# A fused attention, max-out and PReLU kernel: another order of the gate units in the three planned batches

## The chip, the cores and the metric

The kernel runs on one core of a Trainium2 chip. The metric is the device time of one execution in microseconds. It was measured in three runs of the kernel before: 749.68, 751.30 and 750.57 us, median 750.57 us. The trace shown here is of one further execution of the same kernel.

Five engines work side by side, each through its own list of instructions in the order in which they were issued: TensorE (PE in the rows; its weight loads are PEld), VectorE (DVE), ScalarE (ACT), GpSimd (POOL) and SyncE (SP), which here only starts transfers. They wait for each other by semaphores.

## What is computed

```python
def _attn_ref(q, k, v):                      # 4 batches, 8 heads, 576 tokens, 64 wide
    scores = np.matmul(q, k.transpose(0, 1, 3, 2)) / np.sqrt(D)
    rel = pos[:, None] - pos[None, :]
    mask_local = (rel >= 0) & (rel < 32)                                  # heads 0 to 3
    mask_strided = (rel >= 0) & (pos[None, :] % 32 == pos[:, None] % 32)  # heads 4 to 7
    ...
    return softmax(np.where(masks, scores, -1e9)) @ v
def _moe_ref(x, w1, w2, w3, w_out):          # 2304 tokens, 512 -> 768 -> 512
    h = np.maximum(np.maximum(x @ w1, x @ w2), x @ w3)
    return h @ w_out
def _moe2_ref(x, w_in, w_out, alpha):        # 512 -> 2048 -> 512
    h = x @ w_in
    return (np.maximum(h, 0) + alpha * np.minimum(h, 0)) @ w_out
```

The three run one after the other; the output of the attention, seen as 2304 tokens of 512 features, is the input of the second.

## The kernel before

The program has three stretches. In the first (0 to some 316 us of the trace) the attention of all four batches, the max-out net of batches 0, 1 and 2, and the preparation of all weights are woven together. In the second (`last_net`) the max-out net of batch 3 runs. In the third the PReLU net runs over all tokens. Only the first has its order changed.

**Units of the max-out net.** A batch has 576 tokens in two halves of 288 (`hf` 0 and 1). A *gate unit* `(hf, f, g)` multiplies the 288 tokens of a half with one block of 128 columns (`f`, six of them) of one of the three gate weights (`g`): 12 matmuls at line 580, of 128x128 by 288 columns. After the unit g = 0, ACT copies the result to a tile `t` (L667); after g = 1 and g = 2, DVE takes the greater of result and `t` (L670). Then ACT casts `t` into a tile `h` (L676) and DVE makes its low part (L259). A *mix unit* multiplies all six `h` of a half with 128 columns of the output weights: 18 matmuls at line 602; a half has four. Its result `xo` is copied by ACT (L650) and stored by SP (L613). So a batch has 36 gate units (432 matmuls) and 8 mix units (144).

**Attention.** A batch's attention comes in eight steps. Each has scores (L317 on PE), a mask and a maximum (L325, DVE), exponentials (L332, ACT), a reciprocal (L343, L344, DVE), a scaling (L354 on ACT or L356 on DVE), transposes (L367, PE), a copy (L256, ACT or DVE), values (L392, PE) and a split into `x` (L256 and L259). The attention of batch b + 1 runs between the gate and mix units of batch b.

**Weights.** Each block of weights comes in as double precision (`raw`, L437 on SP), is made into single precision words (L451 on ACT; L455 and L457 on DVE) and split into a high and a low part (L256 on ACT, L259 on DVE). In batch 0 the 18 gate weights are made just ahead of their use. Later ones are sums of blocks (L524, L553, L563) and are written back by SP (L489) through three buffers.

**What sets the order.** Each piece of work is a task with engines, estimated costs, a position, needs and the rings of buffers that it takes from: 8 PSUM banks, 4 tiles `t`, 12 tiles `h`, 11 tiles `x`, 3 store buffers and so on. `Weave.plan` goes through a made-up time with these costs and, at each step, takes the task with the lowest position among those that could start soon; a change of kind of work on PE counts 100 ns in it. So the built order of all engines follows from the positions. `net_tasks` gives the gate and mix units of batch b the positions `b * NUNITS + n`, with n counted through a list: `GATES_FIRST` for batch 0, `GATES` for batch 1, `GATES_THEN` for batch 2. An entry `(hf, f)` stands for its three gate units, a `None` for the four mix units of the next half.

**After the planned part.** `last_net` begins with sums on DVE (L704, L710) into tiles that take over the memory of the store buffers, then the gate units of four blocks `f` (144 matmuls at L580, their maxima at L591), with `make(0)` to `make(7)` between them (L214: eight operands, named T1 to T4). Then come products of six matmuls (L753) on these operands; the fifth one takes T4.

Of the kernel before, what the change touches and what calls it, by code (L numbers as in the profile page):

```python
# [163 lines left out]
def attention_maxout_prelu_kernel(  # L164
# [442 lines left out]
    def store_x2(b, hf, dc, xo):  # L607
        first = b * S + hf * HALF
        done = 0
        while done < HALF:  # L610
# [4 lines left out]

    GATES_FIRST = [(0, 0), (0, 1), (1, 0), (0, 2), (1, 1), (0, 3), (1, 2), (0, 4), (1, 3), (0, 5),
                   (1, 4), None, (1, 5), None]
    GATES = [(0, 0), (0, 1), (0, 2), (1, 0), (0, 3), (0, 4), (1, 1), (0, 5), (1, 2),  # L620
             None, (1, 3), (1, 4), (1, 5), None]
    GATES_THEN = [what for what in GATES if what] + [None, None]
    GATES_LAST = [(hf, f) for f in range(2 * NP // 3) for hf in range(2)]

    def units(gates):
# [281 lines left out]
    for b in range(B - 1):  # L907
        net_tasks(b, (GATES_FIRST, GATES, GATES_THEN)[b])
    weave.run()
# [436 lines left out]
```

## Time and profile before

| | |
|---|---|
| runs | 749.68, 750.57, 751.30 us; median 750.57 us |
| the profiled execution | 749.45 us in all; its span, first to last instruction, 747.7 us |
| PE busy | 732.9 us (98% of the span), 5560 matmuls |
| DVE busy | 640.3 us (86%) |
| ACT busy | 464.5 us (62%) |
| granted TensorE clock | 1.000, mean over the span |

The profiled execution is 1.12 us below the median of the runs. Busy time is the time in which an engine had an instruction in work; matmuls overlap, so a full PE is not one at its peak, and the distance from one matmul's start to the next one's says more than the length of one.

### The profile page before, as it was taken

The numbers are of one execution on the slowest core, as the hardware profiler recorded it, in microseconds if no ns is written. First come the engines' busy times: TensorE is split into PE (matmuls) and PEld (weight loads), VectorE is DVE, ScalarE is ACT, GpSimd is POOL, SyncE is SP. The second block draws the span as 40 slices with busy tenths as digits, with TensorE's granted clock in tenths as the row PEclk, the third lists the DMA queues.
The fourth block names the chain that finished last, engine by engine and source line by source line (L and its number), as shares of the span: only waits on it lengthen the run. The fifth ranks groups of instructions, "written<-read, shape, count | busy, mean of one in ns | idle before, by whom it ended". The sixth has DMA issues, their size and how long they took to land.

```text
span 747.7 us, 16003 instructions
## 1 busy us (share of the span) xinstructions
PE 732.9 (98%) x5560; PEld 710.3 (95%) x5560; DVE 640.3 (86%) x1711; ACT 464.5 (62%) x1254; POOL 28.7 (4%) x42
## 2 busy tenths in 40 slices
PE   5899999999999999999999999999999999999998
PEld 4699999999999999999999999999999999999997
DVE  4899999899898999478868898888989888988896
ACT  5987889568684788423345666634666654556571
POOL 1000000000000000023500000000000000000000
PEclk9999999999999999999999999999999999999999
DMA  7477769996999765779899789999789999867362
GB/s 248 155 244 227 234 206 337 342 342 244 323 318 340 252 219 208 253 267 332 306 319 400 266 293 332 383 401 372 265 286 316 364 401 369 289 236 254 118 201 77
DMA packets 88929, 211.96 MB, mean 283 GB/s; under 512 B 11024, under 2 KB 41232, under 8 KB 88848
## 3 DMA queue, kind: packets, MB, share of 16 engines
q1 hardware_dynamic: 88848, 210.94, 80.4%
q8 instruction: 44, 0.72, 0.4%
q14 instruction: 37, 0.30, 0.1%
HBM read 154.80 MB, written 56.10 MB: 282 GB/s over the span
## 4 chain that ended last, share of the span: by engine, by line
PE 94%; ACT 2%; DMA 2%; DVE 1%; issue 0%; SPq 0%; ACTq 0%; DVEq 0%
PE bank L580 24%; PE ph L1185 23%; PE po L986 15%; PE bank L602 10%; PE bank L753 4%; PE po L992 4%; PE ph L986 3%; PE bank L317 3%; PE bank L392 2%; PE bank L367 2%; PE po L996 2%; ACT e L332 1%; DMA wh<-w 1%; DMA k<-in_kTs 0%; PE po L1185 0%; DMA wo<-w 0%
## 5 line engine op out<-in xcount | busy, mean ns | idle before, releaser
L1185 PE MATMUL ph<-x,w 128*128 128x384 f32 x990 | 200.1, 337 | 0.0
L580 PE MATMUL bank<-x,w 128*128 128x288 f32 x1440 | 197.5, 296 | 0.0
L580 PEld LDWEIGHTS bank<-x,w 128*128 128x128 f32 x1440 | 191.8, 188 | 2.1
L1185 PEld LDWEIGHTS ph<-x,w 128*128 128x128 f32 x990 | 166.3, 188 | 1.0
L986 PE MATMUL po<-w,g 128*128 128x256 f32 x936 | 135.6, 281 | 0.0
L986 PEld LDWEIGHTS po<-w,g 128*128 128x128 f32 x936 | 130.1, 189 | 0.4
L1191 DVE TENSOR_TENSOR c<-ph,c 128x384 f32<-128x384 f32 x165 | 89.5, 555 | 30.5 <-PE ph L1185 27.4
L979 ACT CAST g<-c 128x384 fp32r<-128x384 f32 x93 | 47.0, 505 | 91.1 <-DVE c L1169 51.7
L602 PE MATMUL bank<-h,w 128*128 128x288 f32 x576 | 79.4, 297 | 0.0
L602 PEld LDWEIGHTS bank<-h,w 128*128 128x128 f32 x576 | 76.9, 188 | 0.9
L256 ACT CAST w<-word 128x512 fp32r<-128x512 f32 x100 | 58.0, 590 | 24.8 <-DMA wh<-w 7.9
L332 ACT ACTIVATE e<-e,nm 96x128 f32<-96x128 f32 (+2 forms) x176 | 68.1, 396 | 6.1 <-DVE nm L325 5.9
L259 DVE TENSOR_TENSOR w<-word,w 128x512 fp32r<-128x512 f32 x100 | 63.4, 642 | 9.2 <-ACT w L256 8.9
L1129 ACT ACTIVATE c<-c 128x384 f32<-128x384 f32 x96 | 50.5, 526 | 32.9 <-DVE c L1191 31.8
L1130 ACT ACTIVATE c<-c,nalpha 128x384 f32<-128x384 f32 x96 | 59.2, 617 | 3.1
L1134 DVE SCALAR_TENSOR_TENSOR c<-c 128x384 f32<-128x384 f32 x96 | 53.1, 553 | 6.1 <-ACT c L1130 6.1
L980 DVE TENSOR_TENSOR g<-c,g 128x384 fp32r<-128x384 f32 x96 | 53.0, 552 | 0.9 <-ACT g L979 0.5
L451 ACT ACTIVATE word<-raw 128x512 f32<-128x512 f32 x56 | 37.6, 682 | 14.6 <-DMA raw<-in_w 10.8
L980 DVE TENSOR_TENSOR g<-k,g 128x384 fp32r<-128x384 f32 x72 | 37.2, 558 | 7.5 <-ACT g L979 7.5
L992 PE MATMUL po<-w,g 128*128 128x512 f32 x120 | 43.0, 397 | 0.0
L457 DVE SCALAR_TENSOR_TENSOR word<-raw,word 128x512 uint32<-128x512 uint32 x56 | 38.8, 692 | 1.9
L1169 DVE TENSOR_TENSOR k<-c 128x384 f32<-128x384 f32 x72 | 37.9, 551 | 0.0
(107 smaller groups left out, 939.1 us busy)
## 6 DMA issues: line engine op xcount, KB each, us to landing
w<-wh SPq DMA_DIRECT2D x72, 512.0 KB, 5.3
raw<-in_w SPq DMA_DIRECT2D x50, 512.0 KB, 5.1
w<-wo SPq DMA_DIRECT2D x48, 512.0 KB, 5.8
w<-wp SPq DMA_DIRECT2D x36, 512.0 KB, 6.4
wh<-w SPq DMA_DIRECT2D x24, 512.0 KB, 5.0
xd<-xst SPq DMA_DIRECT2D x28, 384.0 KB, 3.2
x<-xd SPq DMA_DIRECT2D x28, 384.0 KB, 8.2
ws<-w SPq DMA_DIRECT2D x12, 512.0 KB, 5.4
```

What stands on the lines that cost most here:

```text
L256: (nc.scalar.copy if e == "ACT" else nc.vector.tensor_copy)(out_, in_)
L259: nc.vector.tensor_tensor(out=out_, in0=x, in1=y, op=ALU.subtract)
L332: nc.scalar.activation(tl[ek][:nq, j, i, :nk], tl[ek][:nq, j, i, :nk], AF.Exp, bias=tl["nm", u][:nq, j, i:i + 1], scale=-1.0, accum_out=tl ...
L580: nc.tensor.matmul(acc, words["gate", f, g][:, wi, cc * P:(cc + 1) * P], xt[b, cc, hf][:, xi, :], start=n == 0, stop=n == 3 * NCC - 1)
L602: nc.tensor.matmul(acc, words["mix", f][:, wi, dc * P:(dc + 1) * P], st["h", hf, f][:, xi, :], start=n == 0, stop=n == 3 * NF1 - 1)
L980: return g, lambda: nc.vector.tensor_tensor(out=g[:, 1], in0=x, in1=g[:, 0].bitcast(F32), op=ALU.subtract)
L986: nc.tensor.matmul(bank[:, NH * half:NH * (half + 1)], g[:, gi, t * P:(t + 1) * P], w[:, wi, off:off + NH], start=first and i == 0, stop=l ...
L992: nc.tensor.matmul(bank.rearrange("p (s n) -> p s n", n=NH), g[:, 0, t * P:(t + 1) * P], w[:, :, off:off + NH], start=first, stop=last)
L1130: nc.scalar.activation(a, a, AF.Copy, scale=nalpha[:, f:f + 1])
L1134: nc.vector.scalar_tensor_tensor(out=a, in0=h, scalar=0.0, in1=a, op0=ALU.max, op1=ALU.add)
L1185: nc.tensor.matmul(bank, words["h", n, i][:, wi, off + c * P:off + (c + 1) * P], x2h[blk, k, c][:, xi, :], start=m == 0, stop=m == 5)
L1191: nc.vector.tensor_tensor(out=out_, in0=bank, in1=other, op=ALU.add)
```

## The change

The three lists of the planned batches are written in another order. In `GATES_FIRST` and `GATES` a `None` stood between gates of the second half; now both `None` stand last. `GATES_THEN` had both last already, and has another order of the gates alone.

```diff
-    GATES = [(0, 0), (0, 1), (0, 2), (1, 0), (0, 3), (0, 4), (1, 1), (0, 5), (1, 2),
-             None, (1, 3), (1, 4), (1, 5), None]
+    GATES = [(0, 0), (1, 0), (0, 1), (0, 2), (1, 1), (0, 3), (1, 2), (1, 3), (0, 4), (0, 5), (1, 4),
+             (1, 5), None, None]
```

The number of matmuls on PE (5210 as issued), and the set of transfers on SP (555), are the same in both programs. From the last mix unit on, PE's list is the same in both. Line numbers after the lists are greater by one in the changed kernel.

PE's list where batch 1 begins, which is the end of batch 0's mix and the first gates of batch 1. Before:

```order
L602 MATMUL bank<-h,w 128x288 x72
L580 MATMUL bank<-x,w 128x288 x96
L367 MATMUL bank<-ident,e 108x108 x6
L580 MATMUL bank<-x,w 128x288 x48
L367 MATMUL bank<-ident,e 126x126 x4
L392 MATMUL bank<-pt,v 64x108 x6
L580 MATMUL bank<-x,w 128x288 x48
L392 MATMUL bank<-pt,v 64x126 x4
L367 MATMUL bank<-ident,e 108x108 x6
L317 MATMUL bank<-k,q 126x126 x4
L580 MATMUL bank<-x,w 128x288 x48
```

And now:

```order
L602 MATMUL bank<-h,w 128x288 x72
L580 MATMUL bank<-x,w 128x288 x60
L317 MATMUL bank<-k,q 108x108 x6
L580 MATMUL bank<-x,w 128x288 x36
L317 MATMUL bank<-k,q 126x126 x4
L580 MATMUL bank<-x,w 128x288 x12
L367 MATMUL bank<-ident,e 108x108 x6
L580 MATMUL bank<-x,w 128x288 x36
L367 MATMUL bank<-ident,e 126x126 x4
L392 MATMUL bank<-pt,v 64x108 x6
L317 MATMUL bank<-k,q 108x108 x6
L580 MATMUL bank<-x,w 128x288 x48
```

The first scores of the next batch stood within the mix of batch 0 before; now they stand by themselves between gates.

DVE's list in batch 0 between the fifth weight block (w_885) and the sixth (w_928 before, w_926 now). Before:

```order
L259 TENSOR_TENSOR w_885<-word_852,w_885 128x512
L259 TENSOR_TENSOR h_906<-t_760,h_906 128x288
L455 TENSOR_SCALAR word_908<-word_908 128x512
L457 SCALAR_TENSOR_TENSOR word_908<-raw_850,word_908 128x512
L670 TENSOR_TENSOR t_789<-bank_910,t_789 128x288
L259 TENSOR_TENSOR w_928<-word_879,w_928 128x512
```

And now:

```order
L259 TENSOR_TENSOR w_885<-word_852,w_885 128x512
L671 TENSOR_TENSOR t_789<-bank_887,t_789 128x288
L259 TENSOR_TENSOR h_905<-t_760,h_905 128x288
L259 TENSOR_TENSOR w_926<-word_879,w_926 128x512
L259 TENSOR_TENSOR h_930<-t_789,h_930 128x288
```

The two steps that make the words of the seventh block stood ahead of the sixth block's low part, and stand behind it now.

SP's list at the end of the planned part: the stores of the last weight sums (wo7, wp) and of the mix results of batch 2 (x2). Before, xo_4917 is the fifth of the batch's eight results and xo_4971 the seventh:

```order
L489 DMA wo7_0_120<-w_4938 128x1024
L489 DMA wo7_1_121<-w_4942 256x1x256
L489 DMA wp2_3_173<-w_4942 256x1x256
L489 DMA wo7_1_121<-w_4966 256x1x256
L489 DMA wp0_3_165<-w_4966 256x1x256
L613 DMA x2_3_71<-xo_4917 128x96
L613 DMA x2_4_72<-xo_4917 128x192
L613 DMA x2_3_71<-xo_4944 128x96
L613 DMA x2_4_72<-xo_4944 128x192
L613 DMA x2_3_71<-xo_4971 128x96
L613 DMA x2_4_72<-xo_4971 128x192
L489 DMA wp1_3_169<-w_4995 256x1x256
```

And now, where xo_4930 is the sixth result and xo_4989 the last:

```order
L613 DMA x2_3_71<-xo_4930 128x96
L613 DMA x2_4_72<-xo_4930 128x192
L489 DMA wo7_0_120<-w_4960 128x1024
L489 DMA wo7_1_121<-w_4987 256x1x256
L489 DMA wp2_3_173<-w_4987 256x1x256
L489 DMA wo7_1_121<-w_5009 256x1x256
L489 DMA wp0_3_165<-w_5009 256x1x256
L613 DMA x2_3_71<-xo_4962 128x96
L613 DMA x2_4_72<-xo_4962 128x192
L613 DMA x2_3_71<-xo_4989 128x96
L613 DMA x2_4_72<-xo_4989 128x192
L489 DMA wp1_3_169<-w_5019 256x1x256
```

The five stores from wo7_0 on stood ahead of the fifth result, and stand behind the sixth now.

## Rows read from the trace of the kernel before

**Rows 1.** The page: the span, busy time by engine, the chain that ended last.

```profile
span 747.7 us, 16003 instructions
...
PE 732.9 (98%) x5560; PEld 710.3 (95%) x5560; DVE 640.3 (86%) x1711; ACT 464.5 (62%) x1254; POOL 28.7 (4%) x42
...
PE 94%; ACT 2%; DMA 2%; DVE 1%; issue 0%; SPq 0%; ACTq 0%; DVEq 0%
```

**Rows 2.** Windows: stretch, its length, busy us (instructions) by engine, clock, DMA share, GB/s.

```profile
25.00:50.00 25.00, 22.69 (x206) 19.89 (x207) 23.78 (x104) 25.00 (x102) 0.00 (x0) 1.00 0.67 218
...
125.00:150.00 25.00, 25.00 (x193) 25.00 (x192) 20.33 (x46) 15.73 (x43) 0.00 (x0) 1.00 0.94 333
```

**Rows 3.** PE's waits, whole span: us in total, times, longest us.

```profile
PE bank L317 <- DMA k<-in_kTs: 5.9, 2, 4.5
...
PE bank L367 <- DVE e L356: 1.9, 3, 0.7
...
PE bank L317 <- ACT pt L256: 0.3, 1, 0.3
```

**Rows 4.** PE's timeline, 38 to 310 us: start, length, merged instructions.

```profile
103.71 1.55 PE L317 MATMUL bank<-k,q 64*96 64x128 f32 x24
105.19 5.06 PE L602 MATMUL bank<-h,w 128*128 128x288 f32 x36
...
131.47 12.86 PE L580 MATMUL bank<-x,w 128*128 128x288 f32 x96
144.17 0.72 PE L367 MATMUL bank<-ident,e 108*108 108x108 f32 x6
144.66 6.62 PE L580 MATMUL bank<-x,w 128*128 128x288 f32 x48
151.12 0.59 PE L367 MATMUL bank<-ident,e 126*126 126x126 f32 x4
...
160.81 6.62 PE L580 MATMUL bank<-x,w 128*128 128x288 f32 x48
167.36 0.90 PE L317 MATMUL bank<-k,q 64*96 64x128 f32 x12
168.19 1.88 PE L580 MATMUL bank<-x,w 128*128 128x288 f32 x12
```

**Rows 5.** PE's timeline where it waits within batch 1.

```profile
212.81 0.71 PE L317 MATMUL bank<-k,q 64*126 64x126 f32 x8 [0.26 <-ACT pt L256]
```

**Rows 6.** PE's timeline, the first 240 matmuls of gates.

```profile
38.45 32.11 PE L580 MATMUL bank<-x,w 128*128 128x288 f32 x240
```

**Rows 7.** DVE's timeline in batch 0: the low parts of blocks five and six.

```profile
48.58 0.69 DVE L259 TENSOR_TENSOR w<-word,w 128x512 fp32r<-128x512 f32 x1
49.18 0.45 DVE L259 TENSOR_TENSOR h<-t,h 128x288 fp32r<-128x288 f32 x1
...
51.10 0.68 DVE L259 TENSOR_TENSOR w<-word,w 128x512 fp32r<-128x512 f32 x1
```

**Rows 8.** DVE's timeline where the last net begins, up to its last operands.

```profile
312.42 0.43 DVE L259 TENSOR_TENSOR w<-word,w 128x256 fp32r<-128x256 f32 x1 [1.48 <-ACT w L256]
319.17 1.56 DVE L704 TENSOR_TENSOR xs<-x 128x288 f32<-128x288 f32 x4 [6.33 <-DMA wp<-w]
...
336.90 0.82 DVE L214 TENSOR_TENSOR x<-t,x 128x288 fp32r<-128x288 f32 x2
```

**Rows 9.** PE's timeline there: the last net's gates and its first products.

```profile
316.24 19.20 PE L580 MATMUL bank<-x,w 128*128 128x288 f32 x144
335.28 10.00 PE L753 MATMUL bank<-x,w 128*128 128x288 f32 x74
```

**Rows 10.** SP's timeline there: the issue of the last weight store.

```profile
316.61 0.52 SPq L489 DMA_DIRECT2D wp<-w  x1
```

**Rows 11.** DMA issues, whole span: count, KB each, median us to landing.

```profile
w<-wp SPq DMA_DIRECT2D x36, 512.0 KB, 6.4
...
wp<-w SPq DMA_DIRECT2D x24, 256.0 KB, 3.2
```

More of the change, by code (lines that the diff above doesn't have):

```diff
@@ L614, in store_x2 @@
             done += nn
-    GATES_FIRST = [(0, 0), (0, 1), (1, 0), (0, 2), (1, 1), (0, 3), (1, 2), (0, 4), (1, 3), (0, 5),
-                   (1, 4), None, (1, 5), None]
-    GATES = [(0, 0), (0, 1), (0, 2), (1, 0), (0, 3), (0, 4), (1, 1), (0, 5), (1, 2),
-             None, (1, 3), (1, 4), (1, 5), None]
-    GATES_THEN = [what for what in GATES if what] + [None, None]
+    GATES_FIRST = [(0, 0), (1, 0), (0, 1), (1, 1), (0, 2), (0, 3), (1, 2), (1, 3), (0, 4), (1, 4), (0, 5),
+                   (1, 5), None, None]
+    GATES = [(0, 0), (1, 0), (0, 1), (0, 2), (1, 1), (0, 3), (1, 2), (1, 3), (0, 4), (0, 5), (1, 4),
+             (1, 5), None, None]
+    GATES_THEN = [(0, 0), (0, 1), (0, 2), (1, 0), (1, 1), (0, 3), (1, 2), (0, 4), (1, 3), (1, 4), (0, 5),
+                  (1, 5), None, None]
     GATES_LAST = [(hf, f) for f in range(2 * NP // 3) for hf in range(2)]
```

## The prediction

> **What bounds the kernel now.** I read the page first: PE is busy for 732.9 of 747.7 us, and 94% of the chain that ended last is PE [rows 1]. The windows say where it is not: in 25 to 50 us it lacks 2.3 us, and from 50 us on the windows are full, as the one at 125 to 150 us, at a granted clock of 1.00, the upper of the two levels (2.4 GHz) [rows 2]. DVE has 20 to 24 of 25 us there, so it is close to being a second bound, but it is not the one that is waited for. The list of PE's waits confirms this: its largest entry is 5.9 us for the first keys, and the only wait after the first gate at 38.45 us [rows 6] is one of 0.26 us for the copy `pt` [rows 3, 5]. The change leaves everything ahead of that gate as it is. So in the planned part, 38 to 316 us, PE has 0.26 us to win from better timing, and what the change does to the time must come from three things: how much time PE's own work takes in the new order, new waits inside the batches, and new waits at the seam to the last net. Behind the seam every engine has its old list.
>
> **PE's own work in the new order.** The matmuls are the same, but PE changes between gates or mix (288 columns, 128 rows) and attention (64 to 128 columns) at other places. The timeline prices this from one start to the next. 96 gates behind a mix and ahead of transposes take 144.17 − 131.47 = 12.70 us, 132.3 ns each [rows 4]. 48 gates with scores on both sides take 167.36 − 160.81 = 6.55 us where 48 x 132.3 ns is 6.35: two edges with scores or values cost 0.20 us, 0.10 each. 48 gates between transposes take 151.12 − 144.66 = 6.46, half of that. One step of scores alone takes 168.19 − 167.36 = 0.83 us, two in one piece 105.19 − 103.71 = 1.48: a piece that is cut in two costs 0.18 more. Now the count, from the two lists of PE between the first gate and the last net: 32 visits to attention before, 37 now. Edges with scores or values go from 43 to 53, edges with transposes stay 21. Pieces of scores go from 19 to 20, pieces of values from 19 to 20, those of transposes stay 20. So 10 x 0.10 + 2 x 0.18 = **1.36 us more** (for a cut of values I take the price of one of scores). The excerpt of PE's list at batch 1's start shows where: scores that shared a visit within the mix now stand alone between gates. Nothing covers this, since PE has no idle time there.
>
> The Trainium skill ("TensorE: Matmul & The Clock Gate", Single matmul latency) gives a single warm matmul (398 + N)/2.4 ns, that is, 166 ns beside its columns. Were each of the ten edges to empty the array once, the first part would be 1.66 us in place of 1.0 by that page, and the sum 0.66 us higher; the row of 48 gates has 0.10 per edge, and I go by the row.
>
> **The wait that goes.** The 0.26 us stand where scores follow two steps of transposes and need a bank back [rows 5]. In the new list these scores stand elsewhere, between gates, so **−0.26 us**.
>
> **Weights in batch 0.** Gates take 12 x 132.3 ns = 1.59 us per unit from 38.45 us on [rows 6]. In PE's lists the blocks are first used by units 0, 2, 4, 5, 7, 9, 10, 11, 13, 15, 16, 17, 21 ... before, and 0, 2, 4, 6, 7, 8, 12, 13, 14, 15, 16, 17, 24 ... now. Only the sixth is wanted earlier: at unit 8, 51.2 us, not unit 9, 52.8. Its low part ended at 51.10 + 0.68 = 51.78 [rows 7], which would be 0.6 us late. But DVE's list has changed as well: behind the fifth block's end at 48.58 + 0.69 = 49.27 stand a maximum, an `h` (0.45 each) and then the sixth block (0.68), so it ends at 50.85, 0.4 us before it is wanted. Bounds 0 and 0.6; I take **0**. The others are wanted at the same unit or later, and what is queued behind (blocks ten to twelve, at the same units as before) keeps its pace, since DVE has lost no work and gained none.
>
> **The seam to the last net.** Here a wait is ready in the trace. DVE's first sum of the last net starts at 319.17 us, after 6.33 us without work, when a weight store has landed [rows 8], issued by SP at 316.61 [rows 10], so 2.5 us before. From there to the last operand T4, at 336.90 + 0.82 = 337.72, DVE goes through a fixed list. PE wants T4 in its fifth product: 335.28 + 4 x 6 x 0.1323 = 338.46 us [rows 9]. So the margin is 0.74 us; beyond it, PE waits as long as the store is late. In the new program SP's five stores from wo7_0 on stand behind the sixth mix result, not the fourth, and DVE's first sum waits for the last two of these five (its semaphores; the very last store now holds back a load instead). The mix ends at 316.24 and a unit takes 18 x 0.1323 = 2.38 us, so the sixth result is there at 311.5; with ACT's copy (0.4 us, an estimate from the like-sized 0.45 of DVE) and two stores ahead at 0.52 each [rows 10], the five start at 312.9 and the fifth is issued at 312.9 + 4 x 0.52 = 315.0, complete at 315.5. It lands 2.5 us later if it flies like the last one before (318.0: no later than now, nothing lost), 3.2 us later by the median of such stores (318.7), and up to 6.4 later by the slower of the two groups shown, loads of twice the size (321.9: 2.7 late, of which PE feels 2.0) [rows 11]. Behind the store DVE holds the maxima of the last net's gates, and these hold banks; but T4's margin is the first to go. I take 1.0 late, between the median and the far end because five stores follow each other closely, so **+0.3 us**, bounds 0 and 2.0.
>
> **Other waits in the batches.** Each of the 24 attention steps has its chain DVE, ACT, DVE, PE at another place among the gates. Lower bound 0 (−0.26 is counted). Upper bound: the longest wait of this kind anywhere, in the start-up where little covers it, is 0.7 us [rows 3]; one for each batch makes 2.1. In 24 steps the trace has one wait, of 0.26, so I take **0**.
>
> **Sum.** 1.36 − 0.26 + 0.3 = +1.4 us on the profiled execution's 749.45 us (span 747.7 and 1.75 around it), 750.85. The median of the runs stands 1.12 us above this execution, so **752.0 us**, 0.19% more than 750.57. 0.2%, 1.5 us, is about what a measurement of this kernel can tell from no change, so this is just within.
>
> **Rivals.**
> - *The seam decides* (chance 0.25). The stores land over 1.1 us late, so that PE waits over 0.4 us: from there on the kernel is slower by over 0.2%. At the far bound, 750.57 + 1.1 + 2.0 = 753.7. For it: the margin of 0.74 is small. Against it: DVE's sums no longer wait for the very last store.
> - *One wait in each batch* (0.15): 0.26 to 0.7 three times, 752.5 to 753.8. For it: DVE is nearly full, so that a chain that stands badly has nothing to catch up with. Against it: one such wait in three batches so far.
> - *Edges empty the array* (0.05): the dearer price of the rule above, 752.6. Against it stands the row of 48 gates.
> - *Visits cost nothing* (0.05): PE's price per edge is made up elsewhere, and only the 0.26 go: 750.3. Against it: from 50 us on PE has no idle time in which to hide anything.
> - *Faster* (0.05): consecutive units now share weights more often. If PE then skipped loads, it would gain; but it has one load for each of its 5560 matmuls [rows 1], and the program still issues each. Apart from that 0.26 us is all there is to win, and only scatter would make it more.
>
> **How the numbers follow.** My forecast as summed has 0.45; its own range is 751.3 to 752.1, +0.7 to +1.5. With the case of visits that cost nothing, 0.50 within 0.2%; with the seam, the waits and the dear edges, 0.45 slower; 0.05 faster. The range that leaves out 0.2 goes down to 750.7, into the case of free visits, and up to 753.7, the far end of the seam.
>
> **What would show it.** In the changed kernel's timeline, 48 gates between scores should again take 6.55 us, and the last net's first gate should start 1.1 us later, at 317.3. DVE's sixth low part should end before PE's ninth unit begins, with no gap in the run of 240 gates. PE should have a gap of some tenths of a us four products behind the last net's gates, and DVE's first sum should start 3 to 4 us behind PE's last-net gates (2.9 now). The prediction is wrong if PE's waits between 38 and 316 us exceed 0.5 us, if that gap exceeds 0.7, or if the gates start the last net no later than now: the last would say that edges are not what the rows make of them.

## The result, and the profile after

Six runs of the changed kernel took 755.91 to 758.78 us, median 757.18; six of the kernel before, on the same chip, 749.49 to 751.30, median 750.48. The ratio is 1.0092, interval 1.0076 to 1.0109: 6.7 us slower, where 752.0 us, within 0.2% of before, had been forecast. The profiled execution took 758.47 us, its span 756.7 us, 9.0 us more than that of [rows 1]. It stands 1.3 us above the median of its kernel and the profiled one before 1.0 below that of its own, so the profiles show some 2 us more loss than the medians.

The page of the changed kernel: span, busy time, the chain that ended last.

```profile
span 756.7 us, 16006 instructions
...
PE 737.5 (97%) x5560; PEld 713.2 (94%) x5560; DVE 639.5 (85%) x1711; ACT 464.5 (61%) x1252; POOL 28.5 (4%) x42
...
PE 85%; DMA 6%; ACT 4%; POOL 1%; DVE 1%; issue 1%; SPq 0%; ACTq 0%; DVEq 0%; POOLq 0%
```

PE was 94% of the chain and is 85%; DMA went from 2 to 6% and ACT from 2 to 4%. So somewhere the end now runs through a transfer and through ACT. PE is also *busy* 4.6 us longer with the same 5560 matmuls, so some matmuls got slower. The list of PE's waits says where the first of the two is (us in total, times, longest):

```profile
PE bank L317 <- DMA k<-in_kTs: 5.7, 2, 4.7
PE ph L1186 <- ACT xo L810: 4.1, 1, 4.1
...
PE bank L317 <- DMA k<-in_kTl: 0.4, 1, 0.4
PE bank L602 <- DVE h L741: 0.2, 1, 0.2
```

The first row answers to the first of [rows 3] and is nearly the same (5.9 there). The second is new: one wait of 4.1 us, at line 1186, for an `xo` copy of ACT. Line 1186 is the first product of the third stretch, the PReLU net; it is nowhere in the prediction. A product here is six matmuls into one PSUM bank, a part of the memory that TensorE writes its results to; the row of 12 matmuls at 394.57 holds the first two products. PE's timeline from the planned part on:

```profile
169.82 6.62 PE L580 MATMUL bank<-x,w 128*128 128x288 f32 x48
176.37 0.90 PE L317 MATMUL bank<-k,q 64*96 64x128 f32 x12
...
318.02 19.20 PE L580 MATMUL bank<-x,w 128*128 128x288 f32 x144
337.06 33.80 PE L754 MATMUL bank<-x,w 128*128 128x288 f32 x252
370.69 2.32 PE L602 MATMUL bank<-h,w 128*128 128x288 f32 x16
373.25 17.20 PE L602 MATMUL bank<-h,w 128*128 128x288 f32 x128 [0.24 <-DVE h L741]
394.57 4.21 PE L1186 MATMUL ph<-x,w 128*128 128x384 f32 x12 [4.12 <-ACT xo L810]
398.57 2.91 PE L1186 MATMUL po<-x,w 128*128 128x384 f32 x12
401.33 2.25 PE L1186 MATMUL ph<-x,w 128*128 128x384 f32 x12
```

The same place in the kernel before, which [rows 1 to 11] don't reach:

```profile
368.88 19.24 PE L602 MATMUL bank<-h,w 128*128 128x288 f32 x144
387.96 2.24 PE L1185 MATMUL ph<-x,w 128*128 128x384 f32 x12
390.04 2.24 PE L1185 MATMUL po<-x,w 128*128 128x384 f32 x12
392.12 2.24 PE L1185 MATMUL ph<-x,w 128*128 128x384 f32 x12
```

Read from start to start, these rows add up the loss. The first gate starts 0.07 us later (38.52), the last net's gates 1.78 us later than in [rows 9] (318.02), its products again 1.78 later, its mix 1.81 later. The mix takes some 0.5 us longer, with a wait of 0.24 us in it, and ends at 390.45, where a next matmul could start about 0.16 us earlier, as it does in the kernel before. Then come 4.3 us in which PE waits. And the first 24 matmuls take 401.33 − 394.57 = 6.76 us where they took 392.12 − 387.96 = 4.16: another 2.6 us. Together that is 9.2 us; the spans differ by 9.0. Windows of 2 us at this place (length, busy us and instructions of PE, PEld, DVE, ACT and POOL, granted clock, DMA share, GB/s) show what the 2.6 us are:

```profile
390.00:392.00 2.00, 0.44 (x4) 0.21 (x2) 2.00 (x6) 2.00 (x6) 0.00 (x0) 1.00 0.93 293
392.00:394.00 2.00, 0.00 (x0) 0.00 (x0) 0.53 (x2) 0.47 (x2) 0.00 (x0) 0.78 0.96 256
394.00:396.00 2.00, 1.43 (x4) 1.43 (x5) 0.00 (x0) 0.40 (x1) 0.00 (x0) 0.50 1.03 320
...
398.00:400.00 2.00, 2.00 (x8) 2.00 (x7) 0.56 (x1) 0.00 (x0) 0.00 (x0) 0.51 1.03 409
400.00:402.00 2.00, 2.00 (x13) 2.00 (x12) 1.03 (x2) 0.91 (x2) 0.00 (x0) 1.00 1.02 388
```

PE does nothing from 390.45 to 394.57, and within that idle time the granted clock falls from 1.00 to 0.50, the lower of the two levels (1.2 GHz). It stays there up to 400 us: 8 matmuls in 2 us, not 13.

Why does the *first* product wait, whose operands are ready? ACT's timeline of the changed kernel:

```profile
379.57 0.51 ACT L211 CAST x<-xs 128x384 fp32r<-128x384 f32 x1 [4.38 <-DMA xs<-x]
...
391.38 1.13 ACT L810 COPY xo<-bank 128x288 f32<-128x288 f32 x3
394.12 0.40 ACT L810 COPY xo<-bank 128x288 f32<-128x288 f32 x1 [1.61 <-DMA x<-xo]
```

And of the kernel before:

```profile
388.34 0.40 ACT L809 COPY xo<-bank 128x288 f32<-128x288 f32 x1 [0.31 <-DMA x<-xo]
390.05 0.40 ACT L809 COPY xo<-bank 128x288 f32<-128x288 f32 x1 [1.31 <-DMA x<-xo]
```

There too ACT's last copies come late: the last ends at 390.45, 2.3 us behind the mix's end at 388.12. Yet PE's first product did not wait for it. The difference is in the PSUM banks. The third stretch opens two pools of banks in place of the one that the mix used:

```python
ps_o = ctx.enter_context(tc.tile_pool(name="ps_o", bufs=6, space=PSUM, reuse_waits="tile"))
ps_h = ctx.enter_context(tc.tile_pool(name="ps_h", bufs=2, space=PSUM, reuse_waits="tile"))
```

so `ps_h`, from which the first two products take their banks, is always banks 6 and 7, whereas the mix results go round a ring whose order follows from the order of all tasks before. The banks of the last eight mix results, oldest first, as built:

```
kernel before    1 6 0 4 7 2 5 3     first product: bank 6, the seventh from the end
changed kernel   3 5 4 0 1 2 7 6     first product: bank 6, the last
```

The same 144 matmuls in the same order, but the first product now writes over the very last mix result, and must wait until ACT has copied it.

### The profile page after: what moved, and what is told of

Its sections match the earlier page's. It is cut to its first block, busy times and chain, and to the rows that moved or that the text cites. A ratio compares the mean times of both kernels' runs of the same rounds, so it can differ in the third digit from the quotient of the medians.

```text
span 756.7 us, 16006 instructions
## 1 busy us (share of the span) xinstructions
PE 737.5 (97%) x5560; PEld 713.2 (94%) x5560; DVE 639.5 (85%) x1711; ACT 464.5 (61%) x1252; POOL 28.5 (4%) x42
## 4 chain that ended last, share of the span: by engine, by line
PE 85%; DMA 6%; ACT 4%; POOL 1%; DVE 1%; issue 1%; SPq 0%; ACTq 0%; DVEq 0%; POOLq 0%
PE bank L580 23%; PE ph L1186 23%; PE po L987 15%; PE bank L602 8%; PE po L993 4%; PE ph L987 3%; PE bank L317 3%; PE bank L392 2%; PE bank L367 2%; DMA xs<-x 2%; PE po L997 2%; ACT e L332 2%; DMA xd<-xst 1%; DMA k<-in_kTl 1%; POOL xst L214 1%
```

## The experiments

The theory: **the lists moved the ring's end, and the first product's bank became that of the last copy; the copy is late anyway, and behind the idle time the clock is lower.** The rival: **the new lists make the preparation of the third stretch late, whatever the banks.** All times are medians with that of the kernel before in the same series; waits and clocks are those of the profiled executions.

### Other banks for the first product

`after_split`, the changed kernel with

```diff
-    ps_o = ...tile_pool(name="ps_o", bufs=6, space=PSUM, reuse_waits="tile"))
+    ps_oa = ...tile_pool(name="ps_oa", bufs=3, space=PSUM, reuse_waits="tile"))
     ps_h = ...tile_pool(name="ps_h", bufs=2, space=PSUM, reuse_waits="tile"))
+    ps_ob = ...tile_pool(name="ps_ob", bufs=3, space=PSUM, reuse_waits="tile"))
+    class Halves:
+        n = 0
+        def tile(self, *args, **kw):
+            self.n += 1
+            return (ps_oa, ps_ob)[self.n % 2].tile(*args, **kw)
+    ps_o = Halves()
```

> The changed kernel with its six banks po split into two pools of three, one allocated ahead of ph and one behind, so that ph takes PSUM banks 3 and 4 in place of 6 and 7. Bank 3 holds the oldest of the last eight mix results, bank 4 the third oldest. Theory (the stall at the third stage is a matter of which bank the ring ended at): the first PReLU product follows the mix directly, at about 390.4 us, with no wait for an xo copy; the granted clock stays at 1.00; the 4.1 us of wait and the 2.6 us of slow products go, 757.2 - 6.7 = 750.5 us. ACT's copy of the first product still stands behind the last xo copy (394.1 us, before 390.05), so up to 1.5 us may come back as small waits: 750.5 to 752. Rival (the work that prepares the third stage is late through the new lists, whatever the banks): PE still waits about 4 us there and the time stays near 757.

Measured: 752.81 us against 750.63, ratio 1.0033 (1.0014 to 1.0051). PE's timeline:

```profile
389.25 2.24 PE L1196 MATMUL ph<-x,w 128*128 128x384 f32 x12
391.33 2.25 PE L1196 MATMUL po<-x,w 128*128 128x384 f32 x12
394.56 2.35 PE L1196 MATMUL ph<-x,w 128*128 128x384 f32 x12 [0.98 <-ACT c L1206]
...
398.55 1.32 PE L1196 MATMUL ph<-x,w 128*128 128x384 f32 x6 [0.59 <-DVE c L1202]
```

No wait ahead of the first product, no slow matmuls, two thirds of the loss gone. The waits of 0.98 and 0.59 us are of the kind that had been allowed for, but the time is 0.8 us above the range, and some 1 us of it is the planned part, which the expected figure left out. The longer wait is explained by ACT's list: ACT's copy of the first product stands behind the last `xo` copy, and it holds the bank that the fifth product needs.

`before_split`, the same edit on the kernel before.

> The kernel before with the same split of pools. Bank 3 now holds the last mix result. Theory (bank): the first product waits for the last xo copy, which ends at 390.05 + 0.40 = 390.45 us, while the mix is done at 388.0, so a wait of 2.5 us with the same release, and up to 2.6 us more for products at the lower clock: 753 to 755.6 us. Rival (the new lists are late): nothing changes, 750.5 us.

Measured: 754.11 us against 750.63, ratio 1.0044 (1.0025 to 1.0063). Nothing in the order of work was changed, and the stall is there, with the clock behind it (0.50 in the windows from 392 to 398 us):

```profile
369.72 19.24 PE L602 MATMUL bank<-h,w 128*128 128x288 f32 x144
392.31 4.21 PE L1195 MATMUL ph<-x,w 128*128 128x384 f32 x12 [3.35 <-ACT xo L809]
```

The two runs cross: one edit takes the stall out of the new lists and puts it into the old ones. The rival is out as the main cause.

`after_hfirst`, the changed kernel with the two pools' lines swapped, so that `ps_h` is banks 0 and 1, fourth and fifth of the eight:

```diff
-    ps_o = ...tile_pool(name="ps_o", bufs=6, space=PSUM, reuse_waits="tile"))
     ps_h = ...tile_pool(name="ps_h", bufs=2, space=PSUM, reuse_waits="tile"))
+    ps_o = ...tile_pool(name="ps_o", bufs=6, space=PSUM, reuse_waits="tile"))
```

> The changed kernel with the pool ph allocated ahead of po, so that ph takes banks 0 and 1 (the fourth and fifth of the last eight mix results) and po starts with 2 and 7 (sixth and seventh) and 6 (the last). Theory (bank): no wait for the first two products; the third and fourth need banks that were copied at 391.4 to 392.5 us, at or shortly after the time they are wanted; 750.5 to 752.5 us, clock 1.00. Rival (late lists): about 757.

Measured: 752.05 us against 750.63, ratio 1.0011 (0.9989 to 1.0033). One wait for an `xo` copy is left, 0.2 us, ahead of the second product, and two for DVE's `c` of 0.8 us in all; the clock stays at 1.00.

### One list at a time

Each is the kernel before with one or two of the three new lists, and `ps_h` again in banks 6 and 7: `gates_only` has the new `GATES`, `first_only` the new `GATES_FIRST`, `then_only` the new `GATES_THEN`, `no_gates` the new `GATES_FIRST` and `GATES_THEN`. The edit of the first (`GATES_THEN` is written out, since it was made from `GATES`; its order is the old one):

```diff
-    GATES = [(0, 0), (0, 1), (0, 2), (1, 0), (0, 3), (0, 4), (1, 1), (0, 5), (1, 2),
-             None, (1, 3), (1, 4), (1, 5), None]
-    GATES_THEN = [what for what in GATES if what] + [None, None]
+    GATES = [(0, 0), (1, 0), (0, 1), (0, 2), (1, 1), (0, 3), (1, 2), (1, 3), (0, 4), (0, 5), (1, 4),
+             (1, 5), None, None]
+    GATES_THEN = [(0, 0), (0, 1), (0, 2), (1, 0), (0, 3), (0, 4), (1, 1), (0, 5), (1, 2),
+                  (1, 3), (1, 4), (1, 5), None, None]
```

> Only batch 1 has its new list; batch 2 keeps the old one, so the stores at the first seam and DVE's first sum should be as in the kernel before. The ring again ends so that the first product's bank (6) holds the last mix result. Theory (bank): a stall at the third stage of about 2.5 us (the last xo copy as long after the mix as before) with the lower clock behind it, on top of a part of the edges' 1.4 us: 753 to 756.5 us. Rival (late lists): with the old list in batch 2 nothing is late there, so about 751.

> Only batch 0 has its new list. The ring of banks ends otherwise: the first product's bank (6) holds the fourth result from the end, the second's (7) the third from the end. Theory (bank): no wait at the third stage and the clock at 1.00; what is left are the planned part's edges, 43 to 48 with scores or values, 21 to 28 with transposes and four more pieces, which the rows price at 5 x 0.10 + 7 x 0.05 + 4 x 0.18 = 1.6 us, so 751 to 752.5 us. Rival (any new list makes the third stage's preparation late): 754 to 757.

> Only batch 2 has its new list. The first product's bank (6) holds the third result from the end, the second's (7) the last. Theory (bank): the first product follows the mix, the second waits for the last copy: that copy ends 2.5 to 4.9 us behind the mix in the traces so far, less the 1.04 us of the first product, so a wait of 1.4 to 3.8 us, some of it with slow products behind it: 752 to 756 us. Rival (bank does not matter): 750.5 to 751.5.

> Batches 0 and 2 have their new lists, batch 1 the old one. The first product's bank (6) holds the second result from the end, the second's (7) the last. Theory (bank): the first product waits some tenths to 2 us, the second for the last copy, together 1.4 to 3.8 us, and the clock may fall behind it: 753 to 757 us with the planned part's edges. Rival (bank does not matter): 751 to 752.

The banks as built and what the profiles show (wait: sum for `xo` copies at the first two products; clock: the lowest of the windows of 2 us from 390 to 402 us):

```
              banks of the last eight    bank 6 / 7, from the end   wait us  clock   median us  before
gates_only    3 7 4 1 0 2 5 6            last / seventh             4.4      0.50    756.87     750.63
no_gates      3 1 2 4 0 5 6 7            second / last              3.2      0.50    755.32     751.28
then_only     2 4 0 5 1 6 3 7            third / last               2.3      0.52    752.77     751.28
first_only    2 4 0 1 6 7 5 3            fourth / third             0.2      1.00    753.30     751.28
```

The wait goes by the place of the bank in the ring. `gates_only` is the strongest of them: two of the three lists are the old ones, and nearly the whole loss is there, since its ring also ends in bank 6 (ratio 1.0081, 1.0050 to 1.0113). Its wait is 4.4 us, not the 2.5 expected, and its time 0.4 us above the range: DVE's first sum is 4.08 us behind the gates there as well, although batch 2 has its old list. `no_gates` is slower by 1.0046 (1.0027 to 1.0064). In the medians `then_only` can't be told from the kernel before (1.0022, 0.9997 to 1.0047): seven of its ten executions took 751.3 to 753.5 us at a mean clock of 1.000, three 755.8 to 756.6 at a lower one, and the profiled one is among the three. Its profile, with the longer wait at the second product, shows where the stall goes:

```profile
390.69 1.32 PE L1186 MATMUL ph<-x,w 128*128 128x384 f32 x6 [0.41 <-ACT xo L810]
393.85 2.10 PE L1186 MATMUL ph<-x,w 128*128 128x384 f32 x6 [1.84 <-ACT xo L810]
```

`first_only` came out at 753.30, ratio 1.0022 (1.0004 to 1.0040), above the 751 to 752.5 expected, and not through banks. Its loss is at the *first* seam, the one that the prediction had examined:

```profile
315.46 19.20 PE L580 MATMUL bank<-x,w 128*128 128x288 f32 x144
334.50 3.35 PE L754 MATMUL bank<-x,w 128*128 128x288 f32 x24
339.41 5.76 PE L754 MATMUL bank<-x,w 128*128 128x288 f32 x27 [1.56 <-ACT x L211]
```

DVE's first sum starts at 321.68 there, 6.22 us behind the gates (2.93 in [rows 8, 9]), and the fifth product waits 1.6 us for ACT's cast of T4. The clock falls here too, to 0.50 in the window of 340 to 342 us: the 27 matmuls behind the wait take 5.76 us, where 27 x 0.1323 is 3.57, and the 252 in all 371.82 − 334.50 = 37.32 us (33.60 before). That is the mechanism of the rival "the seam decides" in a kernel with one of the three lists, and with the slow matmuls its price in this profile, 3.7 us, is above the 2.0 of its far bound.

### The late copy, and the clock

`after_xo`, the changed kernel with two more buffers, so that the last two results don't wait for an older store to land:

```diff
+            xop.append(pool(xox, "xo", 2))
...
-                xo = tp.tile([P, HALF], F32, tag="t", name="xo")
+                xo = (xop[0] if hf and dc > 1 else tp).tile([P, HALF], F32, tag="t", name="xo")
```

> The changed kernel with two more buffers xo, for the last two mix results of the last net, so that ACT's last xo copy no longer waits 1.61 us for the landing of an older store. The bank of the first product is as in the changed kernel. Theory (bank, and a copy that is late): the last copy ends at about 392.9 us instead of 394.5, the wait falls from 4.1 to about 2.5 us, and the time by 1.6 us or more (up to 2.6 more if the clock then stays up): 753 to 755.6 us. Rival (the wait is ruled by the loads or the lists, not by this copy): 757.

Measured: 753.93 us against 750.90, ratio 1.0036 (1.0019 to 1.0052). The bank is as unlucky as before, the wait is 1.9 us instead of 4.1, and ACT's last four copies stand together from 389.25 us on with no wait between them. The clock falls all the same, to 0.51 in 392 to 394 us:

```profile
392.00:394.00 2.00, 2.00 (x8) 2.00 (x7) 0.29 (x1) 0.43 (x1) 0.00 (x0) 0.51 1.01 337
```

```profile
390.60 3.01 PE L1189 MATMUL ph<-x,w 128*128 128x384 f32 x12 [1.90 <-ACT xo L810]
393.40 3.20 PE L1189 MATMUL po<-x,w 128*128 128x384 f32 x12
396.44 2.24 PE L1189 MATMUL ph<-x,w 128*128 128x384 f32 x12
```

`after_fill`, the changed kernel with matmuls in the wait; they add work, and the third product overwrites what they write:

```diff
+        if n == 0:
+            for j in range(24):
+                nc.tensor.matmul(banks[3], words["h", 0, 0][:, 0, :P], x2h[0, 0, 0][:, 0, :],
+                                 start=True, stop=True)
         bank = product(0)
```

> The changed kernel with 24 more matmuls ahead of the first PReLU product, into the bank of the third (its mix result was copied early), with the same weights and 384 columns; the first product still waits for the last xo copy. They add work and leave the result alone, since the third product overwrites them. 24 x 0.173 = 4.2 us of work (2.08 us for 12 products in the kernel before) in a wait of 4.1 us. Theory (the second loss is the clock, which falls because TensorE idles): the first product starts at about 394.6 us as in the changed kernel, the granted clock stays at 1.00, and 24 products take 4.16 us instead of 6.76: 757.2 - 2.6 = 754.6 us. Rival (the products are slow for another reason, a late operand or the transfers that run there): 757 or more.

Measured: 755.19 us against 750.90, ratio 1.0048 (1.0033 to 1.0063), so 4.3 us above the kernel before, where the changed kernel is 6.7 above it: with more work in it, it loses 2.4 us less.

```profile
389.23 4.38 PE L1196 MATMUL po<-x,w 128*128 128x384 f32 x24
394.03 2.35 PE L1186 MATMUL ph<-x,w 128*128 128x384 f32 x12 [0.41 <-ACT xo L810]
396.22 2.24 PE L1186 MATMUL po<-x,w 128*128 128x384 f32 x12
398.30 2.24 PE L1186 MATMUL ph<-x,w 128*128 128x384 f32 x12
```

The first product is as late as before, and its 24 matmuls from there on take 398.30 − 394.03 = 4.27 us, not 6.76; the clock stays at 1.00 in each window. Over the span the mean clock is 0.999 or 1.000 in all eight timed executions; in the six of the changed kernel it is 0.995 to 0.998. So the second loss is the clock, and it goes when the idle time is filled.

`after_xsfirst`, the changed kernel with the tiles of DVE's first sums away from the store buffers' memory:

```diff
-    hw = pool(ctx, "hw", 8, "right")
     xsp = pool(ctx, "xsp", 2, "right")
-    tsp = pool(ctx, "tsp", 3, "right")
     xst = pool(ctx, "xst", 2, "right")
+    hw = pool(ctx, "hw", 8, "right")
+    tsp = pool(ctx, "tsp", 3, "right")
```

> The changed kernel with the tiles xs and xst allocated ahead of the tiles of the sums' weights, so that they no longer take over the memory of the store buffers but that of the raw blocks; bank 6 still holds the last mix result. Theory (the third stage's preparation is late because DVE's first sum at the first seam waits for a store, and the bank passes that on to TensorE): DVE's first sum starts right behind its last low part, about 1.5 us behind the last net's first gate instead of 4.2, the last xo copy comes 1 to 2.7 us earlier against the mix, the wait of 4.1 us falls to 1.4 to 3 us, and the time by 1 to 2.7 us, a little more with fewer slow products: 753 to 756 us. Rival (the lateness arises behind the first seam, in transfers): the sums are early and the wait at the third stage stays at about 4 us, 757. A weight load that now takes the store buffers' memory could cost the last net's products a wait of its own.

Measured: 754.22 us against 751.45, ratio 1.0035 (1.0020 to 1.0050). DVE's first sum, the same in the changed kernel, and PE's first product:

```profile
318.92 1.56 DVE L705 TENSOR_TENSOR xs<-x 128x288 f32<-128x288 f32 x4
```

```profile
322.22 1.56 DVE L705 TENSOR_TENSOR xs<-x 128x288 f32<-128x288 f32 x4 [2.84 <-DMA wp<-w]
```

```profile
391.86 2.37 PE L1186 MATMUL ph<-x,w 128*128 128x384 f32 x12 [2.28 <-ACT xo L810]
```

The sum is 1.28 us behind the gates instead of 4.20 (322.22 − 318.02, in the second row), the last `xo` copy ends 2.2 us behind the mix instead of 4.1, and PE waits 2.3 us. So part of the lateness at the second seam comes from the first, where it cost nothing. It is not a rule for every list: in `then_only` the first sum is 0.23 us behind the gates, and the last copy still ends 3.5 us behind the mix. (In this execution the clock stayed at 1.00; in ten of the eleven timed ones its mean over the span is 0.995 to 0.998, so it fell, and no trace shows where.)

### Both repairs, on either kernel

`after_hfirst_xo` and `before_hfirst_xo`: `ps_h` allocated first, and the two buffers.

> The pool order of after_hfirst together with the two more buffers xo. Theory (what is left there is ACT's copy of the first product, which stands behind the last xo copy): that copy moves from 393.5 to about 392 us, the waits of 0.2 and 0.8 us and the small gaps in the first products go, 752.05 - 1.2 = 750.9 us, which leaves no more than the planned part's 0.9 us and the time of the kernel before within 0.2%. Rival (what is left is the planned part alone): 752.

> The kernel before with both edits (ph allocated first, two more buffers xo). Both theories expect 750.5 us, since no product waits there in its profile. If some runs of the kernel before lose time at this place (its runs reach from 748.5 to 755.4), the median falls by some tenths, to 750.0, and the highest runs vanish.

Measured in one series with 750.90 for the kernel before: 751.09, ratio 0.9999 (0.9984 to 1.0013), and **750.01, ratio 0.9979 (0.9963 to 0.9994)**. The first product follows the mix directly in both (changed lists shown, old lists behind):

```profile
369.23 19.40 PE L602 MATMUL bank<-h,w 128*128 128x288 f32 x144
388.47 2.24 PE L1189 MATMUL ph<-x,w 128*128 128x384 f32 x12
390.55 2.24 PE L1189 MATMUL po<-x,w 128*128 128x384 f32 x12
392.63 2.24 PE L1189 MATMUL ph<-x,w 128*128 128x384 f32 x12
```

```profile
368.97 19.46 PE L602 MATMUL bank<-h,w 128*128 128x288 f32 x144
388.27 2.24 PE L1188 MATMUL ph<-x,w 128*128 128x384 f32 x12
```

With the second seam out of the way the new lists are 1.08 us slower than the old ones in the medians; the two intervals overlap. The old lists with both repairs beat both kernels of the case, by 0.9 and by some 7 us. Where they gain the 0.9 us no profile shows: that of the kernel before has no wait at this place to win. Before the run it had been expected that they would, if some executions of the kernel before stall there; some of them do have a mean clock below 1.00 (0.993 in one of 754.27 us), but where it fell in them no trace shows.

## Why the prediction was wrong

**The step that failed** is the sentence "Behind the seam every engine has its old list", and with it the sum that stops at T4. The lists are the same there, but what they wait for isn't: which PSUM bank a product gets depends on where a ring stands after some hundreds of tiles, and that the three lists do change. The order that I read leaves the numbers of buffers out, so the two programs looked alike. The wait of 4.1 us and the 2.6 us at the lower clock stood in no term, no bound and no rival. The prediction's own test ("wrong if PE's waits between 38 and 316 us exceed 0.5 us, if that gap exceeds 0.7") looked at the wrong stretch, too.

**The second loss has a place as well.** Nothing in [rows 1 to 11] has a stretch at the lower clock, so the prediction had no price for a wait beyond its length. In the profile a wait of 4.1 us cost 6.7 with the slow matmuls behind it. (That this is also the difference of the medians is chance: the profile lost 9.0.)

**PE's own work in the new order: right in direction and roughly in size, but the price per edge doesn't carry over.** The 48 gates between scores again take 176.37 − 169.82 = 6.55 us. From the first gate to the last net's first one there are 279.50 us in the profile after, 0.35 of them a wait for keys, 278.62 or 278.63 in five further profiles with the new lists, and 278.84 in a sixth (`after_xsfirst`). With the old ones it is 277.79 ([rows 6, 9]) and 277.63, and 278.88 in a third, which has two waits for weights more. So about +0.9 us, where 1.36 − 0.26 = 1.1 had been summed; the two repaired kernels differ by 1.08 us. But `first_only`, which the same prices put at 1.6 us (1.3 with the 0.26 that goes there as well), has 278.02 in that stretch, +0.3 us. So the sum agrees for the full change alone, which may be luck; what an edge costs is not shown, and I can't say which edges are cheap.

The price of the Trainium skill ("TensorE: Matmul & The Clock Gate", Single matmul latency), which the page gives for a bf16 matmul, would have put the ten edges 0.66 us higher. By that rule the planned part would have lost an estimated 1.76 us in place of 1.1; the profiles with the new lists have about 0.9, so no run here shows edges at that price.

**The seam to the last net: the mechanism was there, its price was not.** DVE's first sum is 4.20 us behind the gates, 1.27 later than before; "1.0 late" was forecast, "3 to 4 us behind". T4 was ready at 339.95 + 0.82 = 340.77 us, its first half 0.4 us earlier, and the fifth product is due at 337.06 + 24 x 0.1323 = 340.24; no row of PE shows a wait (its weight loads wait 0.17 us), the 252 matmuls take 33.63 us from start to start (33.60 before), and they start as long behind the gates as before (19.04 us in both). So +0.3 came out as 0. `first_only` shows the same chain with a wait of 1.6 us and the lower clock behind it, and `after_xsfirst` shows that some of the lateness went to the second seam instead.

**Weights and other waits.** The run of 240 gates takes 70.74 − 38.52 = 32.22 us here, some 0.3 more than before (31.94). The row of its weight loads on the page has a wait as long as that, for a block's low part, DVE's `w`:

```profile
L580 PEld LDWEIGHTS bank<-x,w 128*128 128x128 f32 x1440 | 192.0, 188 | 3.2 <-DVE w L259 0.3
```

It ends at 50.26 us and is for the *fifth* block, whose end the prediction took over from the trace before: there it was 49.27, here 50.20. The sixth ends at 51.81, not 50.85. In the six other profiles with the new lists the run takes 31.84 to 31.87 us, so this loss belongs to one execution. Of the waits in the batches the new list has one, 0.35 us for keys, for the 0.26 us that went. Both are within the bounds of the prediction.

**The late `xo` copy** is what the unlucky bank made visible. The Trainium skill ("PSUM — Partial Sum Buffer", Summary: rules for kernel authors) asks to evacuate PSUM promptly. In this trace a late copy is what the first product waits for: the last result stands complete in its bank from 390.45 us on and is copied by 394.52, behind two casts for the next stretch, three older copies and, for 1.61 us, the landing of an older store; with two more buffers alone PE's wait is 1.9 us.

**What stays open.** Of the 6.7 us, other banks alone took back 4.5 (`after_split`) and 5.3 us (`after_hfirst`), other banks and the copies in time 6.5 (`after_hfirst_xo`); against the old lists with the same repairs 1.1 us is left, which is about what the planned part shows. These are differences of medians between series, each uncertain by one to two us. Why executions of one kernel differ by up to 7 us (748.46 to 755.36 for the kernel before in one series, the slowest at a lower mean clock) stays open, and how the ring comes to end where it does was read from the built programs, not derived.

## What to carry to other kernels

Where one stretch of a program hands its buffers to another, ask for each of the first consumers *which* buffer it takes over and who frees it last; a reordering far upstream can change that with no instruction moved at the seam. Give the first consumers the buffers that have been free longest (here the order in which pools are allocated decides it), and don't let the last copies of a stretch queue behind preparations for the next. Price a stall of the matmul engine with the slow matmuls behind it: here 4.1 us of wait brought 2.6 us more, and a lower clock stands behind the stall in seven of the eight profiles with 1.5 us or more of wait at one of the two seams and nothing to fill it.

## What was not expected of the hardware

The granted clock fell within one idle stretch of 4.1 us, and stayed at 0.50 for the next 5 to 6 us of dense matmuls. How much idle time goes with a fall is not fixed in these runs: behind an idle stretch of 1.56 us it fell to 0.50 (`first_only`, first seam), behind one of 1.90 us to 0.51 (`after_xo`), behind one of 2.28 us it stayed at 1.00 (`after_xsfirst`). With 24 more matmuls in the wait it stayed at 1.00 (`after_fill`), and the kernel with more work was 2.4 us faster, each against the kernel before in its own series.
